# Gate and up weights loaded tile by tile, ahead of the second x chunk

## Chip, cores, metric

One core of one Trainium2 chip. The metric is the device time of one execution in microseconds. The granted clock, below, is the share of its full clock that TensorE was allowed; a bubble is a stretch in which TensorE idles.

## The reference, cut

A token mixer on x of 2048 tokens by 512: a memory-augmented attention in four segments of 512 tokens (32 heads of 16), and a gated feed-forward of width 1792 on the same x, mixed by a sigmoid gate per token.

```python
x = A_x
g = sigmoid((x * gate_w).sum(-1))          # one number per token
a = attention(x, wq, wk, wv, wo, beta)     # softmax inside a segment, memory across segments
gate = x @ W_gate; up = x @ W_up           # 512 -> 1792
b = (relu(gate) * up) @ W_down             # 1792 -> 512
return g * a + (1 - g) * b
```

## The kernel before

The program is a list of operations with reads and writes. A list scheduler inside the kernel gives each engine a fixed order, from modelled durations of operations and modelled landing times of loads. The order is decided when the kernel is built, so a constant of the model can change the order on every engine.

```python
# model of a load, in the scheduler
self.dma_busy = max(self.dma_busy, issued) + op.nbytes / 310.0
op.end = self.dma_busy + (1800.0 if start < 4000.0 else 3200.0)
...
# order of issue on the sync queue; a few go out on ACT's queue
x chunk 0 (4 x 128 KB, lands in hT), wq, wk, wv (4 x 128 KB each)
load("sp", ["braw"], V.braw[:], A_beta.partition_broadcast(128), 8192)     # bias row, 8 KB
load_gu(0)             # first half of the columns of gate, of up: one 896 KB transfer each, rows "(kt p) n -> p kt n"
load("sp", ["g4"], V.g4[:], gate_w.rearrange("(kt p) -> kt p", p=128), 1 << 12)   # gate_w, 1 KB
load_x(1)              # x chunk 1: four transposing loads
load_gu(1)             # second halves
wo, wd ...
```

The chain from the bias row: ACT computes `eb = exp(braw)`; VectorE computes `romgh = eb + 1`, then in its fixed order copies the K projections out of PSUM (`kT`) and masks them (`kp`), and TensorE needs `kp` for the first scores. `gate_w` (tile g4) goes through a small matmul on TensorE, which also stands in a fixed place.

The softmax here doesn't subtract the row's maximum and nothing guards it: scores larger than these inputs give would overflow.

Of the kernel before, what the change touches and what calls it, by code (L numbers as in the profile page):

```python
# [18 lines left out]
def mm(n, k=1):  # L19
    return k * (max(n, 60) / 2.4 + 2.5)  # L20


def t_act(n, psum=True, ap=0):
    return (174.0 if psum else 198.0) + 0.834 * n + 93.0 * ap


def t_dve(n, rate=1):
    return 155.0 + n / rate / 0.96
# [56 lines left out]
class Sched:  # L85
# [152 lines left out]
    def place(self, op, e, start):  # L238
        op.eng = e
        if op.ep is not None and op.role == "w" and op.ep.bank is None:  # L240
            bi, _ = self._bank_choice(op, e)
            prev = self.bank_ep[bi]
            if prev is not None:
                for r in prev.readers:
                    op.preds.append((r, False))
            self.bank_ep[bi] = op.ep
            op.ep.bank = bi
        deps = {}
        for p in self._pred_done(op, e):
            deps[p.stream] = max(deps.get(p.stream, 0), p.idx)  # L250
        self._waits(e, deps)
        occ = op.occs[e]
        if e == "pe":
            if op.mode != self.mode or start > self.now[e] + 60.0:
                occ += SWITCH
            self.mode = op.mode
        if op.dma:
            d = min(range(self.ndma), key=lambda i: (self.dma_end.get(i, 0.0), i))
            st = f"dma{d}"
            if self.cnt[st] > 0:  # L260
                self._waits(e, {st: self.cnt[st]})
            self.cnt[st] += 1
            inc = 16
            issued = start + occ
            self.dma_busy = max(self.dma_busy, issued) + op.nbytes / 310.0
            op.end = self.dma_busy + (1800.0 if start < 4000.0 else 3200.0)
            self.dma_end[d] = op.end
        else:
            st = e
            self.cnt[st] += 1  # L270
            inc = 1
            op.end = start + occ + op.lat
        idx = self.cnt[st]
        self.prog[e].append(("ins", op, st, inc))
        op.stream, op.idx, op.start, op.done = st, idx, start, True
        sn = dict(self.know[e])
        sn[st] = max(sn[st], idx)
        self.snap[st][idx] = sn
        self.now[e] = start + occ
        self.busy[e] += occ  # L280
        self.log.append((start, start + occ, e, op.name))
# [98 lines left out]
def program(sc, nc, T, PL, PA, A_x, A_wq, A_wk, A_wv, A_wo, A_beta, W_g, W_u, W_d, gate_w, out, NSEG, KT, NF, NT, EPS, SCALE):  # L380
    V = type("V", (), T)

    def op(eng, fn, occ, **k):
        return sc.add(Op([(eng, fn, occ)], **k))

    def pe(fn, occ, **k):
        k.setdefault("lat", PE_LAT)
        if k.get("role") == "w":
            k["reads"] = list(k.get("reads", ())) + [f"init{i}" for i in range(4)]
        return op("pe", fn, occ, **k)  # L390

    def dve(fn, occ, **k):
        return op("dve", fn, occ, **k)
# [7 lines left out]
    def dma(eng, fn, nbytes, occ=500.0, **k):  # L401
        return op(eng, fn, occ, dma=True, nbytes=nbytes, **k)

    def A(ep):
        return PA[ep.bank]

    def xt(c):
        return [f"xT{c}_{kt}" for kt in range(KT)] if c else [f"xT0_{i}" for i in range(4)]
# [3 lines left out]
    def load(eng, names, dst, src, nbytes, occ=460.0):  # L412
        (lact if eng == "act" else lsp).append(dma(eng, lambda e, dst=dst, src=src: e.dma_start(dst, src), nbytes, occ=occ, writes=names, name="ld" + names[0]))  # L413
# [3 lines left out]
    for nm, w, src in (("wq", V.wq, A_wq), ("wk", V.wk, A_wk), ("wv", V.wv, A_wv)):  # L417
        for kt in range(KT):
            load("act" if nm == "wq" and kt % 2 else "sp", [f"{nm}{kt}"], w[:, kt, :], src[kt * 128:(kt + 1) * 128, :], 1 << 17)
    wgr = W_g.rearrange("(kt p) n -> p kt n", p=128)  # L420
    wur = W_u.rearrange("(kt p) n -> p kt n", p=128)
    half = (NF // 2) * 128
    hs_ = ((0, half), (half, NF * 128))

    def load_gu(h):
        a, b = hs_[h]
        load("sp", [f"wg{h}"], V.wg[:, :, a:b], wgr[:, :, a:b], 512 * 2 * (b - a))
        load("sp", [f"wu{h}"], V.wu[:, :, a:b], wur[:, :, a:b], 512 * 2 * (b - a))

    def load_x(c):  # L430
        for kt in range(KT):
            lsp.append(dma("sp", lambda e, c=c, kt=kt: e.dma_start_transpose(V.xT[:, kt, c * 512:(c + 1) * 512], A_x[0, c * 512:(c + 1) * 512, kt * 128:(kt + 1) * 128]),
                           1 << 17, occ=1280.0, writes=[f"xT{c}_{kt}"], name=f"ldx{c}_{kt}"))
    load("sp", ["braw"], V.braw[:], A_beta.partition_broadcast(128), 8192)
    load_gu(0)
    load("sp", ["g4"], V.g4[:], gate_w.rearrange("(kt p) -> kt p", p=128), 1 << 12)
    load_x(1)
    load_gu(1)
    load("sp", ["wo"], V.wo[:], A_wo.rearrange("(g p) n -> p g n", p=128), 1 << 19)
    load("sp", ["wd"], V.wd[:], W_d.rearrange("(f p) n -> p f n", p=128), NF * 128 * 1024)  # L440
    sc.queue(0, lact)
# [36 lines left out]
    def warm(n, k, b):  # L478
        def fn(e):
            for i in range(n):  # L480
                ins = e.matmul(PL[:, b, :], lhsT=V.rl[:, 0, 0:128], rhs=V.rl[:, 0, :], start=True, stop=True)
            return ins
        return pe(fn, n * 427, reads=["rl0"], writes=[f"bankL{b}"], name=f"warm{k}")

    xps, xcs = [warm(6, 0, 3)], []
    for i in range(4):
        def fx(e, i=i):
# [8 lines left out]
        else:  # L496
            xcs.append(act(lambda e, d=dst, s_=srcp: e.activation(d, s_, ACT.Copy), t_act(512), reads=[f"bankL{i}"], writes=[f"xT0_{i}"], name=f"xc{i}"))
    xps.append(warm(4, 1, 0))
    sc.queue(0, xps)
    sc.queue(0, [t for t in xcs if t.eng == "dve"])  # L500
# [16 lines left out]
    for part, (t0, t1) in enumerate(((0, 4), (4, NT))):  # L517
# [14 lines left out]
        for a in range(4):  # L532
            for jj in range(4):
# [3 lines left out]
                                            reads=[f"gexp{part}"], writes=[f"gexpT{part}_{a}{jj}"], name="gexpT")))  # L537
# [184 lines left out]
    def ffn(c):  # L722
        pes, evs = [], []
        slots = []
        for f in range(NF):
            eg, eu = Epoch("ffn"), Epoch("ffn")
            h = 0 if f < NF // 2 else 1
            for ep, w, nm in ((eg, V.wg, "wg"), (eu, V.wu, "wu")):
                for k0 in range(0, KT, 2):
                    def fn(e, ep=ep, w=w, f=f, k0=k0):  # L730
                        for kt in (k0, k0 + 1):
                            ins = e.matmul(A(ep)[:, :], lhsT=w[:, kt, f * 128:(f + 1) * 128], rhs=V.xT[:, kt, c * 512:(c + 1) * 512], start=(kt == 0), stop=(kt == KT - 1))  # L732
                        return ins
                    pes.append(pe(fn, mm(512, 2), reads=[f"{nm}{h}"] + xt(c), name=f"{nm}{c}_{f}", ep=ep, role="w2" if k0 else "w"))
            r = rctr[0]
            rctr[0] = (r + 1) % 3
            hs = hctr[0]
            hctr[0] = (hs + 1) % 20
            slots.append(hs)
            evs.append(sc.add(Op([("act", lambda e, ep=eg, r=r: e.activation(V.rl[:, r, :], A(ep)[:, :], ACT.Relu), t_act(512)),  # L740
                                  ("dve", lambda e, ep=eg, r=r: e.tensor_scalar(V.rl[:, r, :], A(ep)[:, :], 0.0, None, ALU.max), t_dve(512))],  # L741
                                 writes=[f"rl{r}"], name=f"relu{c}_{f}", ep=eg, role="r")))
            evs.append(dve(lambda e, ep=eu, r=r, hs=hs: e.tensor_tensor(V.hT[:, hs, :], A(ep)[:, :], V.rl[:, r, :], ALU.mult), t_dve(512), reads=[f"rl{r}"], writes=[f"hT{hs}"], name=f"hm{c}_{f}", ep=eu, role="r"))  # L743
        return pes, evs, slots
# [49 lines left out]
    a, b, c_, d, e_ = proj(0)  # L794
    put(pproj=a, dproj=b, dsb=c_, aphi=d, spk=e_)
    for s in range(NSEG):
        if s > 0:
            a, b, c_ = nd(s)
            put(pnd=a, dnd=b, spa=c_)
        a, b, c_, d = att(s)  # L800
        put(patt=a, exp=b, pool=c_, datt=d)
        if s < NSEG - 1:
            a, b, c_ = mu(s)
            put(pmu=a, dmu=b, poolmu=c_)
            a, b, c_, d, e_ = proj(s + 1)
            put(pproj=a, dproj=b, dsb=c_, aphi=d, spk=e_)
        a, b, slots = ffn(s)
        put(pffn=a, effn=b)
        a, b, c_ = outp(s, slots)
        put(pout=a, eout=b, spo=c_)  # L810
# [28 lines left out]
    n = {id(t) for e in sc.ENGS for q in sc.queues[e] for t in q[1]}  # L839
# [39 lines left out]
```

## Time and profile before

| | before |
|---|---|
| time before the prediction | 277.46 us median of 3 (they are among the 6 below) |
| time with the later runs, made beside the kernel after | 276.96 us median of 6 (276.76 to 277.53) |
| profiled span | 275.6 us |
| TensorE busy | 265.6 us, 96% |
| first projection / first scores / gate matmuls start | 7.04 / 14.99 / 20.58 us |

From the page of the kernel before: span, busy time of TensorE and of its weight loads, and two groups of loads (count, KB of each, median us from issue to landing).

```profile
span 275.6 us, 5342 instructions
...
PE 265.6 (96%) x2169; PEld 116.7 (42%) x2205; DVE 198.6 (72%) x387; ACT 191.5 (70%) x171; POOL 92.3 (33%) x152
...
wg<-in_B_W_gate_dram SPq DMA_DIRECT2D x2, 896.0 KB, 7.4
wu<-in_B_W_up_dram SPq DMA_DIRECT2D x2, 896.0 KB, 9.2
```

2169 matmuls were recorded beside 2205 weight loads; each matmul has one weight load.

From the timeline of the kernel before. Columns: start, time, engine and line, what is done, count, and in brackets the engine's idle time before it and what ended it. SPq is the sync queue issuing loads.

```profile
6.61 0.43 SPq L413 DMA_DIRECT2D braw<-in_A_beta_dram  x1
...
7.09 0.43 SPq L413 DMA_DIRECT2D wg<-in_B_W_gate_dram  x1
7.56 0.51 SPq L413 DMA_DIRECT2D wu<-in_B_W_up_dram  x1
...
8.11 0.45 SPq L413 DMA_DIRECT2D g<-in_gate_w_dram  x1
8.60 8.87 SPq L432 DMA_TRANSPOSE xT<-in_A_x_dram  x4
...
12.96 0.23 ACT L503 ACTIVATE eb<-braw 128x32 f32<-128x32 bf16 x1 [6.55 <-DMA braw<-in_A_beta_dram]
13.22 0.18 DVE L504 TENSOR_SCALAR romgh<-eb 128x32 f32<-128x32 f32 x1 [1.83 <-ACT eb L503]
13.31 0.68 DVE L580 CAST kT<-psA 128x512 bf16<-128x512 f32 x1
...
14.99 0.39 PE L662 MATMUL psL<-qT,kp 32*128 32x512 bf16 x4 [0.88 <-DVE kp L583]
...
18.02 0.17 PE L513 MATMUL psA<-ident,g 4*128 4x4 bf16 x1
...
19.72 1.02 PE L567 MATMUL psA<-xT,wq 128*128 128x512 bf16 x4
...
20.58 0.59 PE L732 MATMUL psA<-xT,wg 128*128 128x512 bf16 x2
```

The bias row, 8 KB, takes until 12.93 us; behind it ACT, VectorE and then TensorE wait, and TensorE idles 0.88 us before the first scores. And the four transposing loads of x chunk 1 occupy the sync queue for 8.87 us. The landings of the last two of them, from the view of that line in a window (last line: us from issue to landing; the later one is issued at 15.93 us):

```profile
L432 SPq DMA_TRANSPOSE xT<-in_A_x_dram x2: 1455/1496/1536, 14.4 to 15.9; - x2
...
DMA to landing us min/median/max: 3.6/4.1/4.6
```

The last one lands at 19.58 us in the trace's landing records.

### The profile page before, as it was taken

The numbers are of one execution on the slowest core, as the hardware profiler recorded it, in microseconds if no ns is written. First come the engines' busy times: TensorE is split into PE (matmuls) and PEld (weight loads), VectorE is DVE, ScalarE is ACT, GpSimd is POOL, SyncE is SP. The second block draws the span as 40 slices with busy tenths as digits, with TensorE's granted clock in tenths as the row PEclk, the third lists the DMA queues.
The fourth block names the chain that finished last, engine by engine and source line by source line (L and its number), as shares of the span: only waits on it lengthen the run. The fifth ranks groups of instructions, "written<-read, shape, count | busy, mean of one in ns | idle before, by whom it ended". The sixth has DMA issues, their size and how long they took to land.

```text
span 275.6 us, 5342 instructions
## 1 busy us (share of the span) xinstructions
PE 265.6 (96%) x2169; PEld 116.7 (42%) x2205; DVE 198.6 (72%) x387; ACT 191.5 (70%) x171; POOL 92.3 (33%) x152
## 2 busy tenths in 40 slices
PE   8989999999999999999999999999999999999995
PEld 4433343534443444444344343444444343444444
DVE  5498989899989999978789875378667055857200
ACT  3099897898697886787679776785867777762112
POOL 4014234334445353435233424332333332420000
PEclk9999999999999999999999999999999999999999
DMA  7999764001101223020013000000110100000011
GB/s 218 295 185 373 226 78 98 4 0 23 40 0 38 42 57 60 21 53 5 2 38 40 1 21 19 21 19 2 38 38 2 38 21 19 2 0 4 0 38 40
DMA packets 28961, 15.30 MB, mean 56 GB/s; under 512 B 20360, under 2 KB 28936, under 8 KB 28936
## 3 DMA queue, kind: packets, MB, share of 16 engines
q1 hardware_dynamic: 28360, 14.43, 21.8%
q10 hardware_dynamic: 576, 0.52, 0.7%
q8 instruction: 17, 0.28, 0.4%
q14 instruction: 8, 0.07, 0.1%
HBM read 8.14 MB, written 2.10 MB: 37 GB/s over the span
## 4 chain that ended last, share of the span: by engine, by line
PE 84%; DVE 6%; ACT 2%; DMA 2%; issue 2%; SPq 2%; DVEq 0%
PE psA L732 34%; PE psA L771 17%; PE psL L662 9%; PE psA L687 7%; PE psA L567 6%; PE psA L764 5%; PE psA L565 5%; DMA braw<-in_A_beta_dram 2%; ACT E L667 2%; SPq L413 2%; DVE hT L743 1%; PE psA L637 1%; PE psA L608 1%; DVE kT L580 1%; DVE kp L583 1%
## 5 line engine op out<-in xcount | busy, mean ns | idle before, releaser
L667 ACT ACTIVATE E<-psL 128x2048 bf16<-128x2048 f32 x80 | 150.0, 1875 | 39.6 <-PE psL L662 39.3
L670 POOL TENSOR_SCALAR_AFFINE_SELECT E<-E 128x512 bf16<-128x512 bf16 x128 | 82.7, 664 | 148.7 <-ACT E L667 146.9
L732 PE MATMUL psA<-xT,wg 128*128 128x512 bf16 x215 | 57.6, 380 | 1.4 <-issue 1.3
L732 PE MATMUL psA<-xT,wu 128*128 128x512 bf16 x217 | 57.9, 380 | 0.8 <-issue 0.6
L771 PE MATMUL psA<-wd,hT 128*128 128x512 bf16 (+1 forms) x228 | 53.5, 367 | 1.1 <-issue 0.8
L743 DVE TENSOR_TENSOR hT<-psA,rl 128x512 bf16<-128x512 f32 x56 | 38.4, 685 | 14.5 <-PE psA L732 13.0
L692 DVE STREAM_TRANSPOSE Tn<-psA 128x512 f32<-128x512 f32 x32 | 21.5, 700 | 19.2 <-PE psA L687 19.1
L662 PE MATMUL psL<-qT,kp 32*128 32x384 bf16 (+3 forms) x512 | 31.7, 301 | 1.3 <-DVE kp L583 0.9
L771 PEld LDWEIGHTS psA<-wd,hT 128*128 128x128 bf16 x238 | 21.5, 98 | 23.5 <-issue 3.9
L732 PEld LDWEIGHTS psA<-xT,wu 128*128 128x128 bf16 x224 | 20.5, 98 | 25.2 <-issue 2.0
L732 PEld LDWEIGHTS psA<-xT,wg 128*128 128x128 bf16 x224 | 20.1, 98 | 25.1 <-issue 3.5
L740 ACT ACTIVATE rl<-psA 128x512 bf16<-128x512 f32 x29 | 17.2, 597 | 13.8 <-PE psA L732 11.3
L662 PEld LDWEIGHTS psL<-qT,kp 32*128 32x128 bf16 x512 | 8.9, 92 | 33.7 <-ACT E L667 17.6
L741 DVE TENSOR_SCALAR rl<-psA 128x512 bf16<-128x512 f32 x27 | 18.4, 683 | 4.4 <-PE psA L732 3.8
L687 PE MATMUL psA<-E,vaug 128*17 128x256 bf16 (+3 forms) x512 | 21.1, 300 | 0.2 <-DVE kT L580 0.2
L781 ACT ACTIVATE osb<-psA,omg 128x512 bf16<-128x512 f32 (+1 forms) x10 | 6.4, 644 | 15.6 <-PE psA L764 11.7
L567 PE MATMUL psA<-xT,wq 128*128 128x512 bf16 x61 | 16.3, 380 | 0.4 <-issue 0.2
L567 PE MATMUL psA<-xT,wk 128*128 128x512 bf16 x62 | 16.4, 380 | 0.1
L764 PE MATMUL psA<-wo,oT 128*128 128x512 bf16 (+1 forms) x65 | 15.8, 366 | 0.4 <-issue 0.3
L565 PE MATMUL psA<-wv,xT 128*128 128x512 bf16 x62 | 15.2, 380 | 0.2 <-issue 0.2
L687 PEld LDWEIGHTS psA<-E,vaug 128*17 128x17 bf16 x512 | 10.5, 90 | 11.2 <-issue 3.6
L583 DVE TENSOR_SCALAR kp<-kT,pm 128x512 bf16<-128x512 bf16 x32 | 12.4, 397 | 1.2 <-PE psL L662 0.8
(71 smaller groups left out, 211.3 us busy)
## 6 DMA issues: line engine op xcount, KB each, us to landing
out_dram<-osb SPq DMA_DIRECT2D x15, 128.0 KB, 1.7
wg<-in_B_W_gate_dram SPq DMA_DIRECT2D x2, 896.0 KB, 7.4
wu<-in_B_W_up_dram SPq DMA_DIRECT2D x2, 896.0 KB, 9.2
wd<-in_B_W_down_dram SPq DMA_DIRECT2D x1, 1792.0 KB, 13.8
wk<-in_A_wk_dram SPq DMA_DIRECT2D x4, 128.0 KB, 4.3
wv<-in_A_wv_dram SPq DMA_DIRECT2D x4, 128.0 KB, 3.7
wo<-in_A_wo_dram SPq DMA_DIRECT2D x1, 512.0 KB, 9.3
hT<-in_A_x_dram ACTq DMA_DIRECT2D x2, 128.0 KB, 2.9
```

Of the source, the lines that this page charges most:

```text
L565: ins = e.matmul(A(ep)[:, :], lhsT=V.xT[:, kt, tok + col * 128:tok + (col + 1) * 128], rhs=w[:, kt, :], start=(kt == 0), stop=(kt == KT - 1))
L567: ins = e.matmul(A(ep)[:, :], lhsT=w[:, kt, col * 128:(col + 1) * 128], rhs=V.xT[:, kt, tok:tok + 512], start=(kt == 0), stop=(kt == KT - 1))
L662: ins = q.matmul(PL[:, jj, o:o + w], lhsT=V.kp[32 * jj:32 * jj + 32, kslot(s, n), 128 * j:128 * j + 128], rhs=V.qT[32 * jj:32 * jj + 32, q ...
L667: acts.append(act(lambda a, e=e: a.activation(V.E[:, e, :, :], PL[:, :, :], ACT.Exp, scale=SCALE), t_act(2048), reads=[f"bankL{b}" for b i ...
L670: pools.append(pool(lambda g, ap=ap: g.affine_select(out=ap, in_=ap, compare_op=ALU.is_ge, fill=0.0, base=0, pattern=[[0, 4], [1, 128]], c ...
L687: ins = q.matmul(A(ep)[32 * jj:32 * jj + 17, c:512], lhsT=V.vaug[:, s % 2, j, 8 * G + 2 * jj + p, :], rhs=V.E[:, e, jj, o:o + w], start=(j ...
L692: ds.append(dve(lambda e, p=p, ep=eps[p]: e.transpose(V.Tn[:, p, :], A(ep)[:, :]), t_dve(512), writes=[f"Tn{p}"], name=f"tr{s}_{G}_{p}", e ...
L732: ins = e.matmul(A(ep)[:, :], lhsT=w[:, kt, f * 128:(f + 1) * 128], rhs=V.xT[:, kt, c * 512:(c + 1) * 512], start=(kt == 0), stop=(kt == K ...
L741: ("dve", lambda e, ep=eg, r=r: e.tensor_scalar(V.rl[:, r, :], A(ep)[:, :], 0.0, None, ALU.max), t_dve(512))],
L743: evs.append(dve(lambda e, ep=eu, r=r, hs=hs: e.tensor_tensor(V.hT[:, hs, :], A(ep)[:, :], V.rl[:, r, :], ALU.mult), t_dve(512), reads=[f" ...
L764: ins = e.matmul(A(ep)[:, 0:c1 - c0], lhsT=V.oT[:, o0 + G, i * 128:(i + 1) * 128], rhs=V.wo[:, G, c0:c1], start=st_ and G == 0, stop=sp_ a ...
L771: ins = e.matmul(A(ep)[:, 0:c1 - c0], lhsT=V.hT[:, slots[f], i * 128:(i + 1) * 128], rhs=V.wd[:, f, c0:c1], start=st_ and f == f0, stop=sp ...
```

## The change

Its intent: let TensorE begin gate and up on the first contraction tiles (a contraction tile is 128 of the 512 weight rows over which a product sums; one step of the program takes two), without waiting for a whole half, and get all these weights in early. Beside that, the scheduler's model of loads and of the second warm-up (matmuls whose result is not used, just ahead of the first projection) is set anew. Cut to its core:

```diff
-            self.dma_busy = max(self.dma_busy, issued) + op.nbytes / 310.0
-            op.end = self.dma_busy + (1800.0 if start < 4000.0 else 3200.0)
+            self.dma_busy = max(self.dma_busy, issued) + op.nbytes / 340.0
+            op.end = self.dma_busy + (1700.0 if start < 16000.0 else 3200.0)
...
-        load("sp", [f"wg{h}"], V.wg[:, :, a:b], wgr[:, :, a:b], 512 * 2 * (b - a))
-        load("sp", [f"wu{h}"], V.wu[:, :, a:b], wur[:, :, a:b], 512 * 2 * (b - a))
+        for nm, w, src in (("wg", V.wg, W_g), ("wu", V.wu, W_u)):
+            for kt in range(KT):
+                load("sp", [f"{nm}{h}_{kt}"], w[:, kt, a:b], src[kt * 128:(kt + 1) * 128, a:b], 256 * (b - a))
...
+    load_gu(1)
     load_x(1)
-    load_gu(1)
...
-        return pe(fn, n * 427, reads=["rl0"], writes=[f"bankL{b}"], name=f"warm{k}")
+        return pe(fn, n * (427 if k == 0 else 260), reads=["rl0"], writes=[f"bankL{b}"], name=f"warm{k}")
...
-    pes.append(pe(fn, mm(512, 2), reads=[f"{nm}{h}"] + xt(c), ...))
+    pes.append(pe(fn, mm(512, 2), reads=[f"{nm}{h}_{k0}", f"{nm}{h}_{k0 + 1}"] + xt(c), ...))
```

More of the change, by code (lines that the diff above doesn't have):

```diff
@@ L419, in program @@
             load("act" if nm == "wq" and kt % 2 else "sp", [f"{nm}{kt}"], w[:, kt, :], src[kt * 128:(kt + 1) * 128, :], 1 << 17)
-    wgr = W_g.rearrange("(kt p) n -> p kt n", p=128)
-    wur = W_u.rearrange("(kt p) n -> p kt n", p=128)
     half = (NF // 2) * 128
@@ L733, in fn @@
                         return ins
-                    pes.append(pe(fn, mm(512, 2), reads=[f"{nm}{h}"] + xt(c), name=f"{nm}{c}_{f}", ep=ep, role="w2" if k0 else "w"))
+                    pes.append(pe(fn, mm(512, 2), reads=[f"{nm}{h}_{k0}", f"{nm}{h}_{k0 + 1}"] + xt(c), name=f"{nm}{c}_{f}", ep=ep, role="w2" if k0 else "w"))
             r = rctr[0]
```

## The prediction

> **What bounds the kernel now.** TensorE. The page gives PE 96% busy, and in the timeline its 512-column matmuls start 0.216 us apart at a granted clock of 1.0; the Trainium skill, "TensorE: Matmul & The Clock Gate" (Wait — 56ns, not 53.3ns?), gives 215.7 ns for a warm stream, and the trace agrees. All 2205 matmuls at their trace spacing make about 248 us; the rest of the span (275.6 us) is 1.3 us before the first matmul, about 4 us of bubbles in the first 15 us, about 0.9 us of bubbles in every 10 us after that (0.1 us on entering and on leaving each group of score matmuls, 0.33 us on leaving a group of attention-times-V matmuls), and 3 us of last eviction and store. In the waits, PE and its weight loads wait for no DMA for over 0.8 us. Gate half 0 landed at 15.25 us and up half 0 at 17.65 us, and PE turned to them at 20.6 us because projections and scores kept it busy until then.
>
> **What the change does.** It adds 12 transfers on the sync queue (16 of 229 KB for 4 of 917 KB, about 0.45 us of issue each). The four transposing loads of x chunk 1 move from 8.6 to about 15 us. The new constants in the scheduler's model of loads and warm-up change the static order of every engine. PE work is the same. I counted the switches that cost bubbles in both orders: 80 groups of scores and 17 exits of 0.33 us in each. So the body has nothing to win or lose beyond about 1 us.
>
> **On the critical path: the first 30 us.**
> - Before, the bias row (braw, 8 KB) lands at 12.93 us, though most of its 16 engines were done by 10.4; ACT's exp waits 6.5 us for it, VectorE's romgh waits for that, and the kT copies stand behind romgh. PE idles about 0.9 us before the first scores at 15.0.
> - After, romgh stands one place earlier, ahead of the fourth qT copy, and a small vaug copy stands between the kT copies. If braw lands as late, the fourth K projection waits too and the first scores start about 0.8 us later (0.60 to 0.69 us for a copy, 0.23 for the small one, from the trace). Cost: 0.8 to 1.2 us.
> - The tiny gate_w transfer is issued behind eight loads and its matmul stands earlier: 0 to 0.7 us of wait.
> - x chunk 1 queues behind 3.7 MB; at the trace's 350 GB/s it lands at 22.5 to 24.6 us. PE first uses it at 25 to 26 us: no wait expected, little margin.
> - Finer loads win nothing, as PE gets to them after 20 us.
>
> **Prediction.** 277.46 + 0.8 = 278.3 us, eight times in ten 276.6 to 279.8. Faster by over 2%: 1%; within 2%: 95%; slower by over 2%: 4%.
>
> **What would show it.** PE busy sum unchanged; gate matmuls start at about 21 us, no earlier; first scores at about 15.8 us; the weights' second half landed by about 20 us; no wait for x chunk 1.
>
> **What would make it wrong.** braw landing by 10.5 us (then about 1 us faster than before); x chunk 1 landing after 26 us (some us slower); a wait in the rescheduled body, on a phi(k) transpose or x chunk 3, that the order alone doesn't show.

## The result

| | before | after |
|---|---|---|
| time, measured side by side | 276.96 us median of 6 | 276.86 us median of 6 (276.54 to 277.33) |
| ratio, 95% interval | | 0.9992 (0.9977 to 1.0007): same |
| profiled span | 275.6 us | 274.8 us |
| first projection / first scores / gate matmuls start | 7.04 / 14.99 / 20.58 us | 6.44 / 13.72 / 19.27 us |

A ratio is the mean time of one kernel's fast runs over that of the other's of the same rounds, so it is not quite the ratio of the medians quoted. The profiled spans overstate the difference: the profile of before fell on one of its longer executions (277.3 us), that of after on its shortest (276.54 us).

The page of the kernel after:

```profile
span 274.8 us, 5394 instructions
...
PE 269.2 (98%) x2205; PEld 116.2 (42%) x2205; DVE 200.1 (73%) x391; ACT 191.2 (70%) x167; POOL 91.4 (33%) x152
...
wg<-in_B_W_gate_dram SPq DMA_DIRECT2D x8, 224.0 KB, 4.9
wu<-in_B_W_up_dram SPq DMA_DIRECT2D x8, 224.0 KB, 5.5
```

PE's share went from 96% to 98% because no matmul record is missing here (2205 of 2205): a second profile of the same kernel, with 2169 records, has PE busy for 265.1 us in place of 269.2. The same artefact is in the prediction: the "0.33 us on leaving a group of attention-times-V matmuls" is about 0.10 us in the trace of after, where every record is there (0.15 us from start to start, less 0.05 for such a matmul). In the trace of before, 15 of the 17 exits have 0.38 us from start to start, which is 0.15 us and one missing matmul of about 0.22 us.

The timeline of the kernel after, the lines that answer to those of before:

```profile
6.47 0.44 SPq L413 DMA_DIRECT2D braw<-in_A_beta_dram  x1
6.96 1.85 SPq L413 DMA_DIRECT2D wg<-in_B_W_gate_dram  x4
...
8.85 2.00 SPq L413 DMA_DIRECT2D wu<-in_B_W_up_dram  x4
...
10.55 0.23 ACT L502 ACTIVATE eb<-braw 128x32 f32<-128x32 bf16 x1 [4.80 <-DMA braw<-in_A_beta_dram]
10.81 0.18 DVE L503 TENSOR_SCALAR romgh<-eb 128x32 f32<-128x32 f32 x1 [0.61 <-ACT eb L502]
10.90 0.38 SPq L413 DMA_DIRECT2D g<-in_gate_w_dram  x1
10.90 0.68 DVE L573 CAST qT<-psA 128x512 bf16<-128x512 f32 x1
...
13.72 0.40 PE L661 MATMUL psL<-qT,kp 32*128 32x512 bf16 x4
...
14.04 1.04 PE L564 MATMUL psA<-wv,xT 128*128 128x512 bf16 x4
...
15.08 5.23 SPq L431 DMA_TRANSPOSE xT<-in_A_x_dram  x4
...
15.73 0.17 PE L512 MATMUL psA<-ident,g 4*128 4x4 bf16 x1 [0.65 <-DMA g<-in_gate_w_dram]
...
19.27 1.03 PE L731 MATMUL psA<-xT,wg 128*128 128x512 bf16 x4
...
24.46 1.03 PE L566 MATMUL psA<-xT,wq 128*128 128x512 bf16 x4
```

The bias row now lands at 10.53 us, and the first scores stand right behind the K projections with no idle time. But TensorE idles 0.65 us for gate_w. The order also changed: before, the first projection of chunk 1 came ahead of the first gate matmuls; now it comes 5 us after them (x chunk 1 lands at 23.83 us, used at 24.46). To compare the two I measure, in each trace, the time from the first projection to the point where the same matmuls are done (before: the first projection of chunk 1; after: the first gate matmul). I call it the start-up time.

| | start-up time | from there to the last weight load |
|---|---|---|
| before, two profiles | 12.68, 12.81 us | 252.72, 252.73 us |
| after, two profiles | 12.83, 12.80 us | 252.15, 252.15 us |

So the start-up time did not change: the bubble before the scores went and the wait for gate_w came. The rest of the new order is 0.58 us shorter; I have not traced that to a single wait. The time from the last matmul's end to the end of the span is 2.76 us before and 3.00 after, which takes 0.24 us of it back. What remains, about 0.3 us, lies between what the two ratios say (0.2 us by 0.9992 here, 0.5 us by 0.9981 when repeated), and neither is clear of noise. The time of the first projection itself is left out, as it scatters more than these differences: over all profiles with the full warm-up it lies between 6.08 and 7.24 us in before's order and between 6.25 and 7.07 us in after's.

### The profile page after: what moved, and what is told of

It is laid out like the page before. It is cut to its first block, busy times and chain, and to the rows that moved or that the text cites. A ratio compares the mean times of both kernels' runs of the same rounds, so it can differ in the third digit from the quotient of the medians.

```text
span 274.8 us, 5394 instructions
## 1 busy us (share of the span) xinstructions
PE 269.2 (98%) x2205; PEld 116.2 (42%) x2205; DVE 200.1 (73%) x391; ACT 191.2 (70%) x167; POOL 91.4 (33%) x152
## 4 chain that ended last, share of the span: by engine, by line
PE 91%; SPq 3%; DVE 2%; DMA 2%; issue 0%; ACT 0%
PE psA L731 37%; PE psA L770 18%; PE psL L661 9%; PE psA L686 7%; PE psA L566 7%; PE psA L564 5%; PE psA L763 5%; SPq L413 3%; DMA g<-in_gate_w_dram 2%; PE psA L607 1%; PE psA L636 1%; PE psA L522 1%; DVE ttmp L585 1%; DVE ek L586 0%; DVE rdm L629 0%
## 5 line engine op out<-in xcount | busy, mean ns | idle before, releaser
L669 POOL TENSOR_SCALAR_AFFINE_SELECT E<-E 128x512 bf16<-128x512 bf16 x128 | 81.3, 653 | 149.1 <-ACT E L666 134.0
L731 PE MATMUL psA<-xT,wu 128*128 128x512 bf16 x224 | 59.9, 380 | 0.0
L731 PE MATMUL psA<-xT,wg 128*128 128x512 bf16 x224 | 59.7, 380 | 0.0
L770 PE MATMUL psA<-wd,hT 128*128 128x512 bf16 (+1 forms) x238 | 54.3, 367 | 0.0
L691 DVE STREAM_TRANSPOSE Tn<-psA 128x512 f32<-128x512 f32 x32 | 21.5, 700 | 13.0 <-PE psA L686 12.9
L731 PEld LDWEIGHTS psA<-xT,wg 128*128 128x128 bf16 x224 | 19.6, 98 | 24.6 <-issue 5.0
L739 ACT ACTIVATE rl<-psA 128x512 bf16<-128x512 f32 x30 | 17.8, 596 | 14.1 <-PE psA L731 14.1
L740 DVE TENSOR_SCALAR rl<-psA 128x512 bf16<-128x512 f32 x26 | 17.8, 684 | 3.2 <-PE psA L731 2.5
L763 PE MATMUL psA<-wo,oT 128*128 128x512 bf16 (+1 forms) x68 | 16.4, 367 | 0.0
L564 PE MATMUL psA<-wv,xT 128*128 128x512 bf16 x64 | 15.5, 380 | 0.2 <-DVE kT L579 0.2
L686 PEld LDWEIGHTS psA<-E,vaug 128*17 128x17 bf16 x512 | 10.5, 90 | 11.0 <-issue 2.1
L779 DVE TENSOR_SCALAR osb<-psA,omg 128x512 bf16<-128x512 f32 x7 | 5.2, 745 | 12.6 <-PE psA L770 12.6
```

What stands on the lines that cost most here:

```text
L564: ins = e.matmul(A(ep)[:, :], lhsT=V.xT[:, kt, tok + col * 128:tok + (col + 1) * 128], rhs=w[:, kt, :], start=(kt == 0), stop=(kt == KT - 1))
L669: pools.append(pool(lambda g, ap=ap: g.affine_select(out=ap, in_=ap, compare_op=ALU.is_ge, fill=0.0, base=0, pattern=[[0, 4], [1, 128]], c ...
L686: ins = q.matmul(A(ep)[32 * jj:32 * jj + 17, c:512], lhsT=V.vaug[:, s % 2, j, 8 * G + 2 * jj + p, :], rhs=V.E[:, e, jj, o:o + w], start=(j ...
L691: ds.append(dve(lambda e, p=p, ep=eps[p]: e.transpose(V.Tn[:, p, :], A(ep)[:, :]), t_dve(512), writes=[f"Tn{p}"], name=f"tr{s}_{G}_{p}", e ...
L731: ins = e.matmul(A(ep)[:, :], lhsT=w[:, kt, f * 128:(f + 1) * 128], rhs=V.xT[:, kt, c * 512:(c + 1) * 512], start=(kt == 0), stop=(kt == K ...
L739: evs.append(sc.add(Op([("act", lambda e, ep=eg, r=r: e.activation(V.rl[:, r, :], A(ep)[:, :], ACT.Relu), t_act(512)), ("dve", lambda e, e ...
```

## The experiments

To tell the parts apart I pinned the order. The scheduler runs on unchanged operations, and only afterwards is a load moved on the sync queue, or sent as several transfers, or several sent as one; a moved load gets a semaphore of its own where that is needed. For each pinned kernel I compared the built program with its parent: the instruction order of TensorE, VectorE, ACT and GpSimd is the same (except where the warm-up is cut). All 12 runs, of ten edited kernels and the two unchanged ones, gave correct results. "Before order" and "after order" name the parent.

### The kernel before once more

No edit. 

> The kernel before, unchanged, for a second profile. Theory A (the late bias row is a property of the large transfer that follows it): the bias row lands at 12 to 13 us again and the first scores start at about 15.0 us. Rival B (it is chance from execution to execution): it lands anywhere between 10 and 13 us, and the first scores start between 14.1 and 15.0 us. Time 276.8 to 277.5 us in either case.

277.04 us (one run). The bias row landed at 12.67 us (12.93 in the first profile), the first scores started at 14.73 us. So the late landing is not chance. x chunk 1's last tile landed at 19.33 us and its projection started at 19.46 us: 0.13 us apart (0.14 us in the first profile, 19.58 and 19.72 us).

### Only the split, before order

```diff
-        load one transfer:  V.wg[:, :, a:b] <- W_g "(kt p) n -> p kt n"
+        for kt in range(4): V.wg[:, kt, a:b] <- W_g[kt * 128:(kt + 1) * 128, a:b]   # one scheduled load, four transfers
```

> The kernel before, with the order of every compute engine pinned; only each half of gate and up is issued as four transfers instead of one. Theory A: the bias row lands at about 10.5 us as in the kernel after, so the first scores start at about 14.1 us, as soon as the K projections end, and the kernel gains 0.5 to 0.9 us (ratio 0.997 to 0.998). Rival B: the landing has nothing to do with the size of the transfer behind it, and neither it nor the time (ratio 0.999 to 1.001) moves other than by chance. Rival C (start-up bubbles are made up for later): the scores start earlier but the time stays the same.

276.09 us median of 6, ratio 0.9959 (0.9944 to 0.9974): a gain of 1.1 us, more than the 0.5 to 0.9 us expected and more than the whole change has. The timeline of this kernel:

```profile
9.91 0.23 ACT L515 ACTIVATE eb<-braw 128x32 f32<-128x32 bf16 x1 [3.25 <-DMA braw<-in_A_beta_dram]
...
14.24 0.40 PE L674 MATMUL psL<-qT,kp 32*128 32x512 bf16 x4
...
18.88 1.02 PE L579 MATMUL psA<-xT,wq 128*128 128x512 bf16 x4
```

The bias row landed at 9.88 us, the bubble before the scores is gone, x chunk 1 landed at 17.97 us, and its projection starts 0.91 us later, when TensorE comes to it. Start-up time 11.64 us against 12.68 and 12.81. TensorE took nothing from having single tiles: in this kernel a gate matmul still waits for all four, and the gate matmuls come after 19.7 us. The gain is in what stands around the weights on the queue: of the 1.03 us less start-up time than in the first profile, 0.95 us is gained by the first scores, where the bubble was, and 0.08 us at x chunk 1. Rival C falls: in all pinned kernels a shift of TensorE's stream at 25 us is carried to the last matmul within 0.02 us.

### The bias row behind the gate tiles, after order

```diff
 sync queue:
-    braw, wg0_0, wg0_1, wg0_2, wg0_3, wu0_0, ...
+    wg0_0, wg0_1, wg0_2, wg0_3, braw, wu0_0, ...
```

> The kernel after, with the order of every compute engine pinned; only the bias row is issued behind the four gate tiles instead of ahead of them. If the prediction's mechanism is right (the fourth copy of qT and the kT copies stand behind romgh, which waits for the bias row), the row lands at 13 to 14 us, the first scores start at landing + 2.9 us, that is 16 to 17 us, and the kernel loses 1.5 to 3 us against the kernel after (ratio 1.005 to 1.01 against the kernel before). Rival C: the bubble is made up for later, and the time stays within 0.3 us of the kernel after.

279.0 us median (277.61 to 281.51), ratio 1.0086 (1.0047 to 1.0125). The timeline:

```profile
12.85 0.23 ACT L507 ACTIVATE eb<-braw 128x32 f32<-128x32 bf16 x1 [6.51 <-DMA braw<-in_A_beta_dram]
...
13.94 1.04 PE L571 MATMUL psA<-xT,wk 128*128 128x512 bf16 x4 [0.45 <-DVE qT L578]
...
15.57 0.39 PE L666 MATMUL psL<-qT,kp 32*128 32x512 bf16 x4 [0.59 <-DVE kp L587]
```

Landing 12.82 us, first scores 15.57 us; the prediction said 15.8 for a landing of 12.9. Both predicted waits are there, for the fourth copy of qT and for kp. The whole start-up is lengthened less than the scores: start-up time is 13.34 us, 0.5 us more than after, because gate_w has landed when its matmul comes (16.86 us) and the wait of 0.65 us for it is gone. The profile is of the quickest of the six runs. Three runs at a clock of 0.999 to 1.0 took 277.61 to 278.07 us, three at 0.988 to 0.994 took 279.94 to 281.51 us, so most of the 1.0086 goes with the clock; why it fell in these three is not shown, as they have no trace. The mechanism of the prediction, the two waits, is right. Its premise, the late landing, was not.

### Only the bias row early, before order

```diff
 sync queue:
-    x0, wq, wk, wv, braw, wg0, wu0, g4, x1, ...
+    x0, wq, braw, wk, wv, wg0, wu0, g4, x1, ...
```

> The kernel before, order of every compute engine pinned; only the bias row is issued right behind the two halves of wq that the sync queue loads, and has a semaphore of its own. It lands by about 8 us. The first scores then start when the K projections end, at about 14.1 us instead of 15.0: ratio 0.996 to 0.998 (0.5 to 0.9 us) if start-up bubbles count in full; 0.999 to 1.001 under rival C.

277.06 us median, ratio 0.9996 (0.9981 to 1.0011). The timeline:

```profile
13.70 0.40 PE L667 MATMUL psL<-qT,kp 32*128 32x512 bf16 x4
...
17.04 0.17 PE L518 MATMUL psA<-ident,g 4*128 4x4 bf16 x1 [0.24 <-DMA g<-in_gate_w_dram]
...
18.89 1.02 PE L572 MATMUL psA<-xT,wq 128*128 128x512 bf16 x4
```

The scores did start right behind the K projections, 1.29 us ahead of the first profile (0.34 us of it because the first projection started earlier). But then TensorE waited 0.24 us for gate_w, and x chunk 1 landed at 18.75 us with its projection at 18.89 us: start-up time 12.19 us, so about half of the bubble came back as two other waits. In the times of the executions no gain was measured; a gain of over 0.53 us is excluded by the interval, and the 0.5 to 0.6 us that start-up time gained lie at its edge. In the profile, part was lost again at the end: from the last matmul to the end of the span it took 3.30 us (2.7 to 3.0 in the others). This kernel's bubble, to which the chain of waits points ("DMA braw" is 2% of it), is not worth its 0.88 us in this order, because gate_w and x chunk 1 stand close behind it.

### After order, large transfers

```diff
-        four transfers for each half of gate and up
+        one transfer for each half, at the place of the first
```

> The kernel after, with the order of every compute engine and of the loads pinned; only the four tiles of each half of gate and up go out as one transfer again. This is the premise of the prediction on record (the new order with the old landing of the bias row). If the size of the transfer behind it holds the bias row back, the row lands at 12 to 13 us, the first scores start at 15.2 to 16 us, and the kernel loses 1 to 2 us against the kernel after: ratio 1.003 to 1.007 against before. If the landing has another cause (the transposing loads that followed the large transfers before), the row lands at about 10.5 us and the time stays with the kernel after (0.998 to 1.001).

278.31 us median, ratio 1.0058 (1.0031 to 1.0085). But not by the bias row. The timeline:

```profile
10.64 0.23 ACT L519 ACTIVATE eb<-braw 128x32 f32<-128x32 bf16 x1 [4.31 <-DMA braw<-in_A_beta_dram]
...
14.04 0.40 PE L678 MATMUL psL<-qT,kp 32*128 32x512 bf16 x4
...
17.43 0.17 PE L529 MATMUL psA<-ident,g 4*128 4x4 bf16 x1 [2.02 <-DMA g<-in_gate_w_dram]
```

The row landed at 10.62 us although a transfer of 896 KB follows it. So theory A, that the large transfer behind it holds it back, is false. The loss is mainly the wait for gate_w, 2.02 us, which is 1.37 us more than in the kernel after; the ratios differ by about 1.8 us. The matmul starts 0.12 us after the first half of up has landed (17.31 us), which was issued ahead of it. The Trainium skill, "DMA: Bandwidth & Descriptors" (Queues, rings and completion order), says that on each DMA engine descriptors are consumed in ring order; a 1 KB load that shows up directly after the 1.8 MB ahead of it agrees.

With the split kernel this makes a table of four, ratios to before:

| | large transfers | split |
|---|---|---|
| before order | 1 | 0.9959 |
| after order (issue order and scheduler constants) | 1.0058 | 0.9992 |

The split gains 0.4% in one order and 0.66% in the other. The rest of the change costs 0.58% with large transfers and 0.33% with split ones. The whole is the sum: nothing. (The four were measured on three occasions; each ratio is to runs of the kernel before made beside it. With the repeated 0.9981 for the kernel after, the 0.33% would be 0.22%.)

### x chunk 1 behind the second halves, before order

```diff
 sync queue:
-    braw, wg0, wu0, g4, x1, wg1, wu1, ...
+    braw, wg0, wu0, g4, wg1, wu1, x1, ...
```

> The kernel before, order of every compute engine pinned; only the four transposing loads of x chunk 1 are issued behind the second half of gate and up. New theory (what bounds the start of the kernel before is x chunk 1: in all profiles of its order with large transfers the first projection of chunk 1 starts 0.13 to 0.14 us after the chunk's last tile lands): the chunk lands at 22.5 to 24.6 us, the projection starts 0.14 us later, and the kernel loses 3 to 5 us (ratio 1.011 to 1.018). Rival (the chunk is not waited for and the coincidence is chance): loss under 0.5 us. The bias row lands at 12 to 13 us if the large transfer is the cause, at about 10.5 us if the transposing loads behind it are.

285.43 us median of 4, ratio 1.0315 (1.0295 to 1.0334): 8.6 us lost, where 3 to 5 were expected. The timeline:

```profile
18.31 0.38 PE L570 MATMUL psA<-wv,xT 128*128 128x512 bf16 x1
...
25.73 1.87 PE L572 MATMUL psA<-xT,wq 128*128 128x512 bf16 x4 [7.04 <-DMA xT<-in_A_x_dram]
27.38 1.06 PE L737 MATMUL psA<-xT,wg 128*128 128x512 bf16 x2
```

The chunk landed at 25.59 us, later than expected, and the projection started 0.14 us after. TensorE waited 7.04 us. The loss is larger than the wait because the clock fell: the granted clock stood at 0.5 from 23.0 to 29.8 us, and the four projections took 1.66 us to the next start, 0.41 us each instead of 0.216. The Trainium skill, "TensorE: Matmul & The Clock Gate" (HAM oscillation — how this bites in real kernels), describes such a fall to half the clock after a wait of more than about 3.4 us; the trace agrees. But a wait that long is not needed: in the kernel split by partitions, below, the clock fell to half after a wait of 2.18 us. So before's order cannot stand a late x chunk 1. Moving the chunk back is only possible with the new order, and that comes from the scheduler's model.

The bias row landed at 10.65 us here. In the two profiles where transposing loads were issued within 2 us behind the row it landed at 12.93 and 12.67 us; in the others with large transfers and the row in its place it landed at 10.62 and 10.65 us. This kernel differs from before, behind the row, only in what follows gate_w on the queue, so it points to the transposing loads close behind the row; it rests on one or two profiles of each order. By what means they hold it back is open.

### Bias row, gate_w and x chunk 1 early, large transfers, before order

```diff
 sync queue:
-    x0, wq, wk, wv, braw, wg0, wu0, g4, x1, ...
+    x0, wq, braw, g4, wk, wv, x1, wg0, wu0, ...
```

> The kernel before, order of every compute engine pinned, large transfers kept; the bias row and gate_w are issued behind wq and x chunk 1 ahead of the gate weights. If the late bias row and the late x chunk 1 are together what the small transfers cured, this gains what the split kernel gained without any split: 0.8 to 1.3 us (ratio 0.995 to 0.997), with the projection of chunk 1 at about 18.9 us or before and no wait for the gate weights that land at about 17 us. If the small transfers help by something else (gate weights tile by tile), it stays within 0.998 to 1.001.

276.07 us median, ratio 0.9980 (0.9964 to 0.9995). Start-up time 11.69 us, like the split kernel's 11.64, with no split: the bubble and the waits for gate_w and x chunk 1 were what the split cured. After it, though, one wait for a weight appears, as the half of up now lands at 20.15 us. The line is of the weight loads on TensorE:

```profile
20.19 0.55 PEld L737 LDWEIGHTS psA<-xT,wu 128*128 128x128 bf16 x4 [0.59 <-DMA wu<-in_B_W_up_dram]
```

TensorE's stream lost 0.27 us by it. So the expectation was met in the start-up but not in the time: the measured 0.2% is less than the 0.3 to 0.5% that I expected, and at the edge of what I had set for the case that single tiles help by something else. The interval does not separate the two; the start-up time does.

### gate_w early, after order

```diff
 sync queue:
-    braw, eight tiles of gate and up, g4, ...
+    braw, g4, eight tiles of gate and up, ...
```

> The kernel after, order of every compute engine pinned; only the tiny gate_w load is issued right behind the bias row instead of behind eight tiles of gate and up. The wait of 0.65 us before its matmul goes, so the kernel gains about 0.6 us against the kernel after: ratio 0.996 to 0.998 against before. If the next wait behind it (scores for the second group wait for ACT) takes the gain back, the ratio stays at 0.999.

276.14 us median, ratio 0.9980 (0.9965 to 0.9994), so better than before, which the kernel after is not clearly. The timeline:

```profile
14.82 0.17 PE L517 MATMUL psA<-ident,g 4*128 4x4 bf16 x1
...
24.00 1.02 PE L571 MATMUL psA<-xT,wq 128*128 128x512 bf16 x4 [0.29 <-DMA xT<-in_A_x_dram]
```

The wait for gate_w is gone, and start-up time falls from 12.8 to 12.12 us. But TensorE then reaches x chunk 1 before it has landed. In the same order the lead over the first profile of after falls there from 0.91 to 0.46 us and stays so to the end. Half of a removed wait came back as the next one.

### The kernel after once more

No edit. 

> The kernel after, unchanged, on the chip of the next three. Ratio 0.998 to 1.001 against before as in the first measurement; the bias row lands at about 10.5 us again if its landing is a property of the order of the loads (no transposing loads close behind it), anywhere from 10 to 13 us if it is chance.

276.76 us median of 6, ratio 0.9981 (0.9953 to 1.0009): same again. The bias row landed at 10.06 us, so its early landing in this order is not chance. One of the runs of before made beside this kernel and the next three took 279.45 us at a granted clock of 0.994, which widens the intervals of these four.

### Split, with bias row and gate_w early

```diff
 sync queue of the split kernel:
-    x0, wq, wk, wv, braw, eight transfers, g4, ...
+    x0, wq, braw, g4, wk, wv, eight transfers, ...
```

> The split kernel (order of the kernel before, four transfers for each half of gate and up), with the bias row and gate_w issued right behind wq. In the trace of the split kernel no wait for a load was left between the first projection and 30 us, so if the first 20 us are fully explained this can gain no more: ratio within 0.0015 of the split kernel's 0.9959. A gain of 0.5 us or more would show a wait on one of the two that was overlooked.

276.35 us median, ratio 0.9962 (0.9934 to 0.9989). Start-up time 11.64 us, as in the split kernel. Nothing was overlooked on these two.

### Split, with a shorter warm-up

```diff
-            for i in range(n):                        # second warm-up: 4 matmuls
+            for i in range(n if k == 0 else 2):       # second warm-up: 2 matmuls
```

> The split kernel with two instead of four warm-up matmuls between the transposition of x chunk 0 and the first projection. In several traces the warm-up ended after the first half of wq had landed (split kernel: projection at 7.24 us, wq's first two tiles there by 5.7 to 6.3 us), so the start should come forward: gain 0 to 0.6 us against the split kernel (ratio 0.9935 to 0.9965), unless the granted clock suffers or x chunk 1 (landed 17.97, used at 18.88) becomes the next wait.

275.90 us median (275.65 to 276.29), ratio 0.9946 (0.9918 to 0.9974). The first projection starts at 6.38 us (7.24 in the split kernel's profile), the granted clock stays 1.0. That the shorter warm-up did this is not shown, as with the full one the first projection started anywhere between 6.08 and 7.24 us. The kernel has the lowest median of all. It and the split kernel beat before, and no run of either was as slow as the fastest of after (275.65 to 276.45 us against 276.54 to 277.36, for the split kernel on other occasions); that it beats the split kernel is not shown, as their intervals overlap.

### Split by partitions instead of contraction tiles

```diff
-    for kt in range(4): w[:, kt, a:b] <- rows kt * 128 to kt * 128 + 127
+    for q in range(4):  w[32 * q:32 * q + 32, :, a:b] <- "(kt p) n -> p kt n" of these 32 partitions
```

> The split kernel, but its four transfers divide the 128 partitions into four groups of 32 and each carries all four contraction tiles, so that the number and the size of the transfers are the split kernel's and the four strided rows of a partition stay in one transfer as in the kernel before. If the number of transfers makes the first halves of gate and up land by 15.8 us instead of 17.4, this one does it too (ratio 0.995 to 0.997, x chunk 1 landed by 18.0 us). If the pattern of rows in one transfer does it, they land at 17 us or later and the ratio is 0.999 to 1.001.

279.7 us median, ratio 1.0075 (1.0040 to 1.0111): slower than with the large transfers, which neither expectation allowed. The first half of up landed at 18.79 us, against 17.65 us with one large transfer and 15.82 us split by tiles. The timeline:

```profile
19.14 0.17 PE L526 MATMUL psA<-ident,g 4*128 4x4 bf16 x1 [2.18 <-DMA g<-in_gate_w_dram]
...
21.60 1.64 PE L580 MATMUL psA<-xT,wq 128*128 128x512 bf16 x4
```

Part of the loss is clock: after the wait of 2.18 us the granted clock stood at 0.5 from 19.42 to 22.83 us, so the four projections took 0.41 us each; five of the six runs have this kernel's mean clock of 0.994, and the one at 1.0 took 278.24 us.

So four transfers of a quarter of the size are not by themselves what helps. Of the two cuts tried, only that by contraction tile does, with 128 neighbouring rows of the weight in a transfer. The cut by partitions has 32 partitions in a transfer in place of 128 as well as the strided rows, so which of the two makes it slow is open.

## Why the prediction was wrong

The time lay in the stated range, near its low end, and "same" was given 95%. The forecast change, +0.8 us, did not come: the measured one is -0.1 us. That the time still fell in the range is owed to its width and to two errors of opposite sign (the bias row landed earlier, and gate_w was waited for in full), not to the mechanism.

- "If braw lands as late": this premise is the step that failed. The prediction put a cost of 0.8 to 1.2 us on it. After, the row landed at 10.53 and 10.06 us instead of 12.93, so the fourth K projection did not wait and the bubble that before has there (0.88 us) vanished. I had named a landing by 10.5 us as what would make me wrong, but took the old landing as the likely case, though the change moves the transposing loads that stood behind the row. The waits it would have met are real: with the row landing at 12.82 us the first scores started at 15.57. But they do not simply add to the wait for gate_w: with the late row that wait was gone, and start-up time grew by 0.5 us.
- "Then about 1 us faster than before" failed too, as the other half of that alternative. The gain on the row was eaten by gate_w. "0 to 0.7 us of wait" for it was right in size (0.65 us in the first profile, 0.78 in the second) but, with the row landing early, belongs fully in the sum.
- "Finer loads win nothing, as PE gets to them after 20 us" was wrong. TensorE indeed gets to the gate weights only at 19.3 us. But loads issued behind the weights land after them, and split by tile the same first halves landed at 15.8 us instead of 17.65. That moved x chunk 1 forward by 1.6 us, and with the bias row's earlier landing (9.88 us) it is worth 1.1 us in before's order.
- "x chunk 1: no wait expected, little margin" held: landed at 23.83 us, inside the predicted 22.5 to 24.6, and 0.63 us before its use.
- "Gate matmuls start at about 21 us, no earlier" and "first scores at about 15.8" were wrong with the premise: 19.27 and 13.72 us. "The weights' second half landed by about 20 us" was nearly right, 20.51 us.
- "0.33 us on leaving a group of attention-times-V matmuls" was misread: one missing record in each of 15 of the 17 exits. "17 exits of 0.33 us in each" falls with it. The bound on the rest of the kernel, about 1 us, held (0.58 us shorter).

Where the split's gain went: the split alone gains 1.1 us in before's order. In the full change, gate_w stands behind eight tiles with its matmul ahead of eight V matmuls, and TensorE waits 0.65 us for it; moving that one load (gate_w early) gives 0.2% against before. I did not run the scheduler's constants and the order of issue apart from each other, so of the 0.33% that both cost beside the split, only gate_w's wait and the limit set by x chunk 1 are shown.

## What to carry to other kernels

In an in-order start-up the waits stand close behind one another, and removing the one that the chain names brings out the next: count the slack of the second and third wait before putting a price on the first. A tiny load that a compute engine waits for is worth trying ahead of the large ones on a queue (it ended the wait for gate_w here; for the bias row alone it gained nothing that could be measured), and a change to big loads is to be judged by what lands behind them, not only by when their own data are needed. Pinning the instruction order while changing one load separates the load's effect from the reshuffling that a scheduler does with it.

## What the Trainium skill lacked or had wrong

- "DMA: Bandwidth & Descriptors" (Rules for kernel authors) advises transfers of 1 MiB and more, and joining small ones. Here the first halves of gate and up, issued from 6.9 to 7.1 us on, had landed by 15.5 to 15.8 us as eight transfers of 224 KB by contraction tile, and by 16.7 to 17.65 us as two of 896 KB with four strided rows per partition. Eight transfers of the same size over 32 partitions each had landed by 18.79 us. The page has no figure that sets four strided rows per partition in one transfer against one row in each of four.
- The same page does not say how long a transposing load can hold its issuing queue behind large transfers. The issue of one took 1.2 to 1.3 us in the kernel after, up to 3.73 us in the kernel before, and 5.46 us behind two more large transfers (x chunk 1 behind the second halves).
- No page that I read says that transposing loads can delay small loads issued ahead of them: the 8 KB bias row landed at 12.7 to 12.9 us with them close behind it and at 10.6 us without, beside the same large transfers.
- No page that I read warns that missing matmul records look like bubbles: 36 of 2205 were missing in the profile of before. Each missing record lengthens the time from start to start by about 0.22 us; as idle time the profile shows 0.16 us of it behind a group of scores or attention-times-V matmuls and 0.05 us inside a stream, 0.11 us in the mean (269.2 us busy with all records, 265.1 with 36 missing, same kernel).
